# K evicted in output order, another unit order, gated loads and more filler matmuls in a fused attention and token-mixing kernel

## The chip, the cores and the metric

The kernel runs on one core of one Trainium2 chip. TensorE (PE) multiplies matrices into PSUM, VectorE (DVE) and ScalarE (ACT) read PSUM and write SBUF, GpSimd (POOL) works on SBUF and issues the input loads, SyncE (SP) issues the other transfers. Each engine works through its own queue in order. The metric is the device time of one execution in microseconds, the median of the runs; smaller is better.

## The reference, cut to what matters

Four batches of eight heads, 768 rows of 64. An 8x8 matrix P per head is normalised five times by rows and columns; it mixes the eight blocks of K and V. Block-local attention follows, then a token-mixing layer on the joined heads.

```python
P = sort_net
for _ in range(5):
    P = P - np.max(P, axis=-1, keepdims=True)
    P = np.exp(P)
    P = P / (np.sum(P, axis=-1, keepdims=True) + 1e-09)
    P = P / (np.sum(P, axis=-2, keepdims=True) + 1e-09)
k_sorted = np.einsum('bhij,bhjcd->bhicd', P, k_b).reshape(B, H, S, D)
v_sorted = np.einsum('bhij,bhjcd->bhicd', P, v_b).reshape(B, H, S, D)
...
scores = scale * np.matmul(q_b, k_sb.transpose(0, 1, 2, 4, 3))
attn = softmax(scores)          # per block of 96 rows
x = np.matmul(attn, v_sb)       # heads joined to [B, 768, 512]
...
wq = x @ w_q
wk = x @ w_k
W_tok = (1 / 8) * np.einsum('bsd,btd->bst', wq, wk)
mixed = np.einsum('bst,btd->bsd', W_tok, x)
out = np.maximum(mixed, 0.0) @ w_out
```

## The kernel before, in words

The whole kernel is a list of small units, written in the string `ORDER`. A unit is a letter, a batch, a number and one last character: `k02A` is unit k of batch 0, part 2, on ACT. A capital letter is a group of matmuls and its last character is the PSUM bank (0 to 7) that it starts at; a small letter is the work on A (ACT), D (DVE), P (POOL) or S (SP) that follows. The program walks the string and issues each unit in that order, so that the string sets the order on every engine's queue. All matmuls are issued by one helper, all plain copies by another, so most rows of the profile carry the helper's line.

For each batch the units are:

- `l`: a load on POOL's queue, which also converts fp32 to bf16: parts 0, 1, 2 are Q, K, V (1.5 MB read, 768 KB written), parts 3 and 4 the weights. Q, K and V have three buffers each (`NIN = 3`), so those of batch 3 wait until batch 0's are read.
- `c`, `i`: the Sinkhorn rounds on 32 rows and the constants. `U`, `b`, `B`, `n`, `u` turn the result into the matrices M that mix blocks (two buffers; batch 0's by DVE, the others by POOL).
- `Q`, `q`: 48 transposes of Q and their eviction into QT.
- `K`, `k`: for a pair of heads, 12 matmuls give the mixed and transposed K in PSUM, laid out as (r, s, i), 6 x 16 x 8; the eviction at the line of `copy` puts it into KT as (i, s, r), so that each block of 96 rows is contiguous. There are four such units in a batch.
- `V`, `v`, `R`: mixed V, its eviction, and a transfer on SP's queue that spreads it into VT.
- `S`, `e`: scores for five pairs of block and heads and their exp into E; seven units. `P`, `r`, `x`: attention times V, the reciprocal of the sums, and the product into X; five units.
- `T`, `t`, `J`, `j`, `d`, `W`, `w`, `G`, `g`, `H`, `h`, `O`, `o`, `y`: the token-mixing layer, transposes, projections, ReLU, the output product and its store.
- `Z`: filler matmuls of zeros, 128x512, whose result nobody reads. The number of matmuls is the number of the unit.

The loop that reads the string takes the second character as the batch and all between it and the last one as the number:

```python
for item in ORDER.split():
    kind, b, n, arg = item[0], int(item[1]), int(item[2:-1]), item[-1]
```

Of the kernel before, what the change touches and what calls it, by code (L numbers as in the profile page):

```python
# [9 lines left out]
BF16 = mybir.dt.bfloat16  # L10
# [5 lines left out]


ORDER = """
l00P l02P l01P i00P i03P i02P l03P l10P l11P l12P l04P l20P l21P l22P c00D Z087 c01D i01D c02D Z067
c03D Q027 Q016 c04D Q005 l30P q02D c05D q00D U004 b00D q01D B007 n01D n00D K020 u00D n11P K032 n10P  # L20
k02A V000 k03A K014 v00D V022 R00S k01D K000 l31P R01S v02A V016 l32P k00D R04S n20P v01A R05S S050
S062 S044 n21P e05A R03S S026 R02S e04A Q101 Q110 e02A q10D S034 q11D Q121 e06A S016 e03A P032 q12D
e01A r03D K120 x03D P024 k12A P016 r02D K112 x02D K100 k11A r01D T025 x01D k10A V122 t02A V110 v12D
T014 v11A K136 t01D R15S P042 R14S k13A S004 R13S V100 r04D x04D R12S e00A S166 n31P v10D S122 e16A
S144 n30P e12A P006 R11S S130 R10S r00D e14A T033 x00D Q222 e13A Q205 q22D T004 q20A S116 t03D S150
Q212 t00D e11A J013 q21D P124 e15A j01D K206 r12D d01S x12D P140 k20A K222 r14D P134 x14D k22A K216
r13D x13D P110 k21A W013 J002 r11D w01A x11D V204 j00A T123 d00S W002 v20D T137 w00A V220 t13A T112
t12D G006 R21S t11A v22D R20S S104 J113 e10A Q312 j11D R25S Q327 R24S q31A P100 d11S q32D K234 r10D
W117 x10D V212 k23A G016 w11A v21D S214 g01A S220 T107 e21A Q306 t10D R22S H012 e22A H004 R23S J107
h01D h00A K320 j10D S232 q30A O015 k32D d10S e23A V326 V310 o01A v32D S202 W104 v31A O025 R35S w10A  # L30
K306 R32S e20A o02D R33S G104 R34S k30A S250 P202 e25A O035 r20D x20D P216 o03A H020 G114 r21D y01S
h02A x21D S262 O005 g11A e26A O041 o00A H112 y00S T200 o04D P244 t20A h11D V306 O051 v30A r24D K332
x24D o05A R30S H126 R31S K314 k33D y02S h12A H100 k31D S242 h10A O157 e24A S314 S360 o15D O136 e36A
e31A P232 o13D S340 O107 r23D e34A x23D P224 o10A S320 O146 r22D e32A x22D T237 o14A S302 T225 t23D
e30A y12S P310 t22D S336 T214 r31D e33A P302 x31D J215 t21A r30D P326 x30D j21A S350 J204 d21S e35A
r32D W215 T303 x32D j20A O122 t30A d20S W204 w21A P330 o12D w20A T313 r33D G207 y11S x33D t31A P344
G217 O116 r34D g21A x34D T327 o11D T335 t32A H220 H212 t33D y10S J304 h22A h21D J315 H200 j30D O257
j31A h20D d30S d31S W316 W305 o25A O244 w30D w31A O205 o24A G307 y22S o20A O214 G317 o21A O225 g31D
y20S H320 O234 o22D h32A H302 H316 o23A O355 h31D h30A y21S O344 O307 O316 o30D o34A o35D O333 o31D
y32S O322 o33D y30S o32A y31S  # L40
"""


# [1 line left out]
def kernel(  # L45
# [11 lines left out]
    nc = tc.nc  # L57
    B, H, S, D = q.shape
    NB = sort_net.shape[-1]
    BLK = S // NB  # L60
    BH = B * H
    P = 128
    R6 = S // P
    SP = BLK // R6
# [16 lines left out]
    sb = ctx.enter_context(tc.tile_pool(name="sb", bufs=1))  # L81
    psp = ctx.enter_context(tc.tile_pool(name="psp", bufs=1, space=bass.MemoryType.PSUM))

    def tiles(name, n, shape, dtype=BF16):
        return [sb.tile(shape, dtype, name=f"{name}{i}") for i in range(n)]
# [16 lines left out]
    QT = tiles("QT", 2, [P, NP, R6, P])  # L102
    KT = tiles("KT", 2, [P, NP, S + P - BLK])
    Vs = tiles("Vs", 2, [P, R6, H, D1])
    VT = tiles("VT", 2, [BLK, NB, H * D1])
    E = tiles("E", 2, [BLK, NT, EW])
    X = tiles("X", 2, [BLK, NB, DM])
# [9 lines left out]
    R = tiles("R", 4, [BLK, 2, 7], FP32)  # L117
# [4 lines left out]
    tmp = sb.tile([BH, NB], FP32, name="tmp")  # L122
    idb = sb.tile([P, P], BF16, name="idb")
    m_p = sb.tile([P, SP], BF16, name="m_p")
    fil = sb.tile([P, 512], BF16, name="fil")

    Pv = Pm[:, 0:NB, :]
# [10 lines left out]
    def copy(e, o, i):  # L138
        if e == "A":
            nc.scalar.copy(o, i)  # L140
        else:
            nc.vector.tensor_copy(o, i)  # L142
# [99 lines left out]
    def flat(bank, nb=2):  # L242
        return PS[:, bank:bank + nb, :].rearrange("p a n -> p (a n)")
# [7 lines left out]
                   M[b % 2][:, h].rearrange("p s i -> p (s i)"))  # L251

    def u_k(b, n, e, bank):
        copy(e, KT[b % 2][:, n, 0:S].rearrange("p (i s r) -> p r s i", i=NB, s=SP),
             flat(bank)[:, 0:S].rearrange("p (r s i) -> p r s i", r=R6, s=SP))


    def u_V(b, n, bank):
# [9 lines left out]
    def u_R(b, n, e):  # L268
        ENG[e].dma_start(out=VT[b % 2].rearrange("(s r) i x -> r s i x", r=R6)[n],
                         in_=Vs[b % 2][:, n].rearrange("p h e -> p (h e)"))  # L270


    def u_S(b, n, bank):
# [16 lines left out]
    def grp(n):  # L290
        u0 = n * AG
        return u0, min(AG, NU - u0) // 2
# [117 lines left out]
    fills = dict(q="Q", k="K", v="V", e="S", r="P", x="P", t="T", j="J", w="W", g="G", h="H", o="O")  # L410
    for item in ORDER.split():
        kind, b, n, arg = item[0], int(item[1]), int(item[2:-1]), item[-1]
        if kind.isupper() and kind not in "R":
            banks[kind, b, n] = int(arg)
            if kind in "UB":
                U["t" if kind == "U" else "bank"] = int(arg)
            fns[kind](b, n, int(arg))
        elif kind in fills:
            src = (fills[kind], b, 1 if kind == "g" else n)
            fns[kind](b, n, arg, banks[src])  # L420
        else:
            fns[kind](b, n, arg)
# [30 lines left out]
```

## Time and profile before

| what | value |
|---|---|
| median of 3 runs | 160.85 us (158.92 to 160.88) |
| the profiled execution's own time | 161.63 us |
| its span, first to last instruction | 159.5 us |
| mean granted TensorE clock | 0.783 |
| loads of Q, K, V | 12, 768 KB each |
| filler matmuls | 14 |

The page gives busy time per engine, the span in 40 slices (tenths), the chain of work that ended last with its shares, and groups of instructions with their busy time, mean duration in ns of one, and the idle time ahead of them with what ended it. In slices of 4 us, DMA is full for the first 60 us, and PE has its longest idle stretches from 10 to 60 us.

### The profile page before, as it was taken

The numbers are of one execution on the slowest core, as the hardware profiler recorded it, in microseconds if no ns is written. First come the engines' busy times: TensorE is split into PE (matmuls) and PEld (weight loads), VectorE is DVE, ScalarE is ACT, GpSimd is POOL, SyncE is SP. The second block draws the span as 40 slices with busy tenths as digits, with TensorE's granted clock in tenths as the row PEclk, the third lists the DMA queues.
The fourth block names the chain that finished last, engine by engine and source line by source line (L and its number), as shares of the span: only waits on it lengthen the run. The fifth ranks groups of instructions, "written<-read, shape, count | busy, mean of one in ns | idle before, by whom it ended". The sixth has DMA issues, their size and how long they took to land.

```text
span 159.5 us, 3288 instructions
## 1 busy us (share of the span) xinstructions
PE 107.3 (67%) x1390; PEld 71.0 (45%) x1399; DVE 87.5 (55%) x130; ACT 101.1 (63%) x95; POOL 26.2 (16%) x37
## 2 busy tenths in 40 slices
PE   6561346197226499626797594859655999999960
PEld 2161335186126378524656443434313686644320
DVE  3888039838231535940447179433994886862360
ACT  3110695289997986799648972993923687553520
POOL 7998751900000600000000000000000000000000
PEclk9959555559855855975559879996975899999998
DMA  2999999999999990000230200415220031435545
GB/s 14 183 201 201 195 204 204 233 242 204 204 204 206 230 217 11 12 4 0 50 96 16 69 5 11 134 48 216 85 116 0 4 132 29 164 123 197 201 188 209
DMA packets 19950, 20.19 MB, mean 127 GB/s; under 512 B 2016, under 2 KB 18400, under 8 KB 19936
## 3 DMA queue, kind: packets, MB, share of 16 engines
q0 software_dynamic: 14064, 10.09, 42.1%
q1 hardware_dynamic: 5872, 9.89, 18.5%
q8 instruction: 11, 0.18, 0.5%
q14 instruction: 3, 0.02, 0.0%
HBM read 20.19 MB, written 6.29 MB: 166 GB/s over the span
## 4 chain that ended last, share of the span: by engine, by line
PE 46%; ACT 21%; DVE 12%; issue 9%; DMA 8%; POOL 1%; DVEq 0%; ACTq 0%; POOLq 0%
PE ps L136 46%; ACT KT L140 17%; DVE KT L142 11%; DMA Kn<-in_k_dram 8%; ACT E L284 3%; DVE Vs L142 1%; POOL Qn L99 1%; POOL Vn L99 1%; ACT ot L140 0%; ACT wk L140 0%; ACT Vs L140 0%; DVE qkT L142 0%; DVEq L142 0%; ACTq L140 0%; POOLq L437 0%
## 5 line engine op out<-in xcount | busy, mean ns | idle before, releaser
L140 ACT CAST KT<-ps 128x768 bf16<-128x768 f32 x11 | 42.4, 4101 | 8.5 <-PE ps L136 8.4
L284 ACT ACTIVATE E<-ps 96x960 bf16<-96x960 f32 (+1 forms) x28 | 24.9, 925 | 12.4 <-PE ps L136 12.0
L136 PE MATMUL ps<-wo,mixT 128*128 128x512 bf16 x87 | 25.5, 418 | 0.9 <-issue 0.5
L316 DVE TENSOR_TENSOR X<-ps,R 96x896 bf16<-96x896 f32 (+1 forms) x20 | 20.1, 1006 | 0.7
L136 PE MATMUL ps<-QT,KT 64*128 64x96 bf16 x256 | 11.4, 237 | 13.2 <-DVE KT L142 8.0
L142 DVE CAST KT<-ps 128x768 bf16<-128x768 f32 x5 | 19.3, 4025 | 0.4 <-PE ps L136 0.4
L136 PE MATMUL ps<-Vn,M 128*128 128x128 bf16 x96 | 10.4, 274 | 13.2 <-ACT KT L140 10.9
L142 DVE CAST Vs<-ps 128x1024 bf16<-128x1024 f32 x7 | 8.8, 1258 | 18.1 <-PE ps L136 18.1
L136 PEld LDWEIGHTS <-KT 64*128 64x128 bf16 x256 | 8.3, 112 | 16.9 <-issue 13.4
L136 PEld LDWEIGHTS <-M 128*128 128x128 bf16 x96 | 8.4, 125 | 14.8 <-issue 14.4
L136 PE MATMUL ps<-M,Kn 128*64 128x128 bf16 x192 | 9.8, 251 | 7.7 <-ACT KT L140 4.8
L136 PE MATMUL ps<-VT,E 96*128 96x65 bf16 x256 | 12.4, 202 | 2.2 <-ACT KT L140 2.0
L136 PEld LDWEIGHTS <-mixT 128*128 128x128 bf16 x96 | 8.5, 103 | 10.7 <-issue 3.0
L142 DVE COPY ot<-ps 128x512 f32<-128x512 f32 x11 | 7.6, 711 | 9.8 <-PE ps L136 9.8
L136 PEld LDWEIGHTS <-E 96*128 96x128 bf16 x256 | 10.7, 103 | 4.8 <-issue 3.4
L136 PE MATMUL ps<-idb,Qn 128*64 128x128 bf16 x192 | 10.5, 292 | 2.8 <-POOL E L183 2.7
L140 ACT COPY ot<-ps 128x512 f32<-128x512 f32 x13 | 7.6, 587 | 6.9 <-PE ps L136 5.0
L136 PEld LDWEIGHTS <-Kn 128*64 128x64 bf16 x192 | 7.2, 127 | 10.5 <-issue 6.9
L216 POOL TENSOR_TENSOR M<-PTR,m_p 128x512 bf16<-128x512 bf16 x6 | 7.7, 1312 | 21.7 <-PE ps L136 21.6
L136 PEld LDWEIGHTS <-Qn 128*64 128x64 bf16 x192 | 9.2, 158 | 4.5 <-DMA Qn<-in_q_dram 3.2
L136 PE MATMUL ps<-idb,X 96*128 96x96 bf16 x128 | 10.0, 235 | 1.3 <-ACT wk L140 1.3
L311 DVE RECIPROCAL R<-ps 96x14 f32<-96x14 f32 (+1 forms) x20 | 4.6, 229 | 10.5 <-PE ps L136 10.4
(64 smaller groups left out, 131.7 us busy)
## 6 DMA issues: line engine op xcount, KB each, us to landing
out_dram<-ot SPq DMA_DIRECT2D x12, 512.0 KB, 2.9
VT<-Vs SPq DMA_DIRECT2D x24, 130.0 KB, 3.9
Qn<-in_q_dram POOLq DMA_DIRECT2D x4, 768.0 KB, 17.3
Vn<-in_v_dram POOLq DMA_DIRECT2D x4, 768.0 KB, 23.3
Kn<-in_k_dram POOLq DMA_DIRECT2D x4, 768.0 KB, 19.8
wo<-in_moe_w_out_dram POOLq DMA_DIRECT2D x1, 512.0 KB, 20.2
qD<-qkT SPq DMA_DIRECT2D x8, 48.0 KB, 1.9
wqk<-in_moe_w_q_dram POOLq DMA_DIRECT2D x1, 64.0 KB, 7.5
```

The lines of the kernel that those rows point to most:

```text
L99: nc.gpsimd.dma_start(out=t[b % NIN].rearrange("p h r d -> p h (r d)"), in_=src[b].rearrange("h (p r) d -> p h (r d)", p=P))
L136: nc.tensor.matmul(o, w, x, is_transpose=t, start=start, stop=stop, skip_group_check=True)
L140: nc.scalar.copy(o, i)
L142: nc.vector.tensor_copy(o, i)
L216: ENG[e].tensor_tensor(out=M[b % 2][:, h0:h1], in0=src.unsqueeze(2).to_broadcast([P, 4, SP, NB]), in1=m_p.unsqueeze(1).unsqueeze(3).to_bro ...
L284: nc.scalar.activation(E[b % 2][:, n, 0:2 * w * BLK].rearrange("p (t a c) -> p a t c", a=2, c=BLK), PS[0:BLK, bank:bank + 2, 0:w * BLK].re ...
L311: nc.vector.reciprocal(rr[b, n][:, :, 0:w], avps(bank, w)[:, :, :, D])
L316: nc.vector.tensor_mul(xo.rearrange("p (a t d) -> p a t d", a=2, d=D), avps(bank, w)[:, :, :, 0:D], rr[b, n][:, :, 0:w].unsqueeze(3).to_br ...
```

## The change

The eviction of K walks the same elements in the order of the output in place of that of the input. The order of all units is another one. Loads after the first four wait for gates: a unit `N` copies one element of a tile into a scrap tile on POOL, so that what stands behind it in POOL's queue goes out only when that tile's unit has run. The queue of loads begins q, k, v where it was q, v, k, and batch 1's K follows at once. There are more filler units: 14 groups with 64 matmuls in place of 2 groups with 14. Evictions are dealt out anew: K 9 on ACT and 7 on DVE (before 11 and 5), Q 6 and 6 (3 and 9), V 6 and 6 (5 and 7), output 16 and 8 (13 and 11), the ReLU 8 and 4 (7 and 5), the projections 2 and 6 (4 and 4), and all 8 of `w` on DVE (1).

```diff
-l00P l01P l02P i00P i03P i02P l03P l10P l11P l12P l04P l20P l21P l22P c00D Z087 c01D i01D c02D Z067
...
+l00P l01P l02P i00P i03P i02P l11P c00D Z087 c01D i01D c02D Z027 c03D Z127 c04D Q026 Q007 q02D c05D
...
+R00S K112 S000 R04S S044 n20P e00A k11D S066 e06A R02S K100 e04A S012 R05S S036 R03S k10A Z1125 Z924
+e03A K120 K134 e01A k12D S026 e02A k13D P002 S050 r00D Z1227 e05A x00D N00x l21P P014 V106 r01D P030
...
+    gate = sb.tile([1, 1], BF16, name="gate")
...
     def u_k(b, n, e, bank):
-        copy(e, KT[b % 2][:, n, 0:S].rearrange("p (i s r) -> p r s i", i=NB, s=SP),
-             flat(bank)[:, 0:S].rearrange("p (r s i) -> p r s i", r=R6, s=SP))
+        copy(e, KT[b % 2][:, n, 0:S].rearrange("p (i s r) -> p i s r", i=NB, s=SP),
+             flat(bank)[:, 0:S].rearrange("p (r s i) -> p i s r", r=R6, s=SP))
...
+    def u_N(b, n, e):
+        t = dict(q=QT, k=KT, v=Vs, e=E, x=X)[e][b % 2]
+        if e == "q":
+            src = t[0:1, 0, 2 * n + 1, P - 1:P]
+        elif e == "k":
+            src = t[0:1, n, S - 1:S]
+        elif e == "v":
+            src = t[0:1, 2 * n + 1, H - 1, D - 1:D]
+        elif e == "e":
+            src = t[0:1, n, 0:1]
+        else:
+            src = t.rearrange("p i m -> p (i m)")[0:1, grp(n)[0] * D:grp(n)[0] * D + 1]
+        nc.gpsimd.tensor_copy(gate, src)
...
-        if kind.isupper() and kind not in "R":
+        if kind.isupper() and kind not in "RN":
```

On ACT, the rows from the start of batch 0 to its first exps. Before (the table of exp is loaded first, Pm is the Sinkhorn matrix; a row with x2 stands for two alike):

```order
L155 ACT_TABLE_LOAD
L155 ACTIVATE Pm<-Pm 32x64 x5
L140 CAST KT_79<-ps 128x6x16x8 x2
L140 CAST Vs_81<-ps 128x8x2x64 x2
L284 ACTIVATE E_85<-ps 96x2x5x96 x3
L284 ACTIVATE E_85<-ps 96x2x2x96
```

And in the changed kernel, the same place on ACT:

```order
L157 ACT_TABLE_LOAD
L157 ACTIVATE Pm<-Pm 32x64 x5
L142 COPY QT_77<-ps 128x4x256
L142 CAST PTR<-ps 128x256
L142 CAST KT_79<-ps 128x768 x2
L142 CAST Vs_81<-ps 128x8x2x64
L142 CAST KT_79<-ps 128x768
L301 ACTIVATE E_85<-ps 96x2x5x96
L301 ACTIVATE E_85<-ps 96x2x2x96
```

One eviction of Q, the copy PTR of the block matrices and a third eviction of K came to ACT there, a V went to DVE, and the write of KT is one run of 768.

On POOL, the rows behind the constants, before (Qn, Kn and Vn are the loaded tiles; M_105 is batch 1's M):

```order
L190 DMA wqk<-in_moe_w_q_dram 128x4x64
L190 DMA wqk<-in_moe_w_k_dram 128x4x64
L99 DMA Qn_67<-in_q_dram 128x8x384
L99 DMA Kn_70<-in_k_dram 128x8x384
L99 DMA Vn_73<-in_v_dram 128x8x384
L192 DMA wo<-in_moe_w_out_dram 128x4x512
L99 DMA Qn_68<-in_q_dram 128x8x384
L99 DMA Kn_71<-in_k_dram 128x8x384
L99 DMA Vn_74<-in_v_dram 128x8x384
L99 DMA Qn_66<-in_q_dram 128x8x384
L216 TENSOR_TENSOR M_105<-PTR,m_p 128x512 x2
```

And in the changed kernel, the same place on POOL, from the second gate on to the loads of batches 2 and 3:

```order
L287 COPY gate<-KT_79 1x1
L100 DMA Vn_73<-in_v_dram 128x8x384
L100 DMA Qn_67<-in_q_dram 128x8x384
L218 TENSOR_TENSOR M_104<-PTR,m_p 128x512 x2
L287 COPY gate<-X_87 1x1
L100 DMA Kn_71<-in_k_dram 128x8x384
L287 COPY gate<-QT_78 1x1
L100 DMA Qn_68<-in_q_dram 128x8x384
L100 DMA Kn_69<-in_k_dram 128x8x384
L194 DMA wo<-in_moe_w_out_dram 128x4x512
L100 DMA Vn_72<-in_v_dram 128x8x384
L100 DMA Qn_66<-in_q_dram 128x8x384
```

Each COPY gate stands ahead of the loads that it holds back: one on batch 0's X, then one on batch 1's QT ahead of five loads. The load of batch 2's V (Vn_74) is still further behind, after a gate on batch 2's E.

More of the change, by code (lines that the diff above doesn't have):

```diff
@@ L18 @@
 ORDER = """
[L19 to L38, printed above, removed]
@@ L39 @@
-y20S H320 O234 o22D h32A H302 H316 o23A O355 h31D h30A y21S O344 O307 O316 o30D o34A o35D O333 o31D
-y32S O322 o33D y30S o32A y31S
+l00P l01P l02P i00P i03P i02P l11P c00D Z087 c01D i01D c02D Z027 c03D Z127 c04D Q026 Q007 q02D c05D
+Q015 Z224 q01A q00D U006 Z423 b00D Z322 B003 n00D u00A Z522 n11P n01D Z622 K010 K032 n10P k01A K024
+k03D Z727 k02A N02k l03P Z1026 V000 V022 v00A K004 v02D V016 k00A N00k l12P l10P Z821 R01S n21P v01D
+R00S K112 S000 R04S S044 n20P e00A k11D S066 e06A R02S K100 e04A S012 R05S S036 R03S k10A Z1125 Z924
@@ new lines @@
+e03A K120 K134 e01A k12D S026 e02A k13D P002 S050 r00D Z1227 e05A x00D N00x l21P P014 V106 r01D P030
+x01D v10A P042 r04D P024 r03D x04D T007 x03D V112 t00A R10S v11A r02D Q106 x02D R11S Q127 T031 q12A
+Q110 q10D T015 t03D q11A N11q l20P l31P l04P l32P l30P T024 V122 t01A S100 n31P v12D S156 t02A J005
+e10A n30P S122 R12S j00D J014 R15S e15A K200 R14S j01D W005 R13S e12A w00D W014 S116 w01D G005 e11A
+K232 G015 k23A K216 g01D k20A k21D S144 P112 e14A P100 r11D K226 x11D P134 k22A r10D Q213 r13D x10D
@@ new lines @@
+S166 Q202 q21A x13D T101 q20A Q220 t10D S134 e16A q22D e13A K322 P146 k32D S250 S214 e25A r14D P122
+x14D e21A K330 r12D S246 d00S x12D k33A K304 e24A k30D S220 T123 T112 e22A t12D K314 S236 t11D T133
+k31A S260 J102 t13D e23A S204 d01S j10D J113 e26A N26e l22P e20A V306 V310 v30D j11A W102 H024 v31A
+W113 w11D V326 w10D h02D G103 v32A H000 d10S R30S Q312 h00D Q325 q31A G113 q32D Q304 g11A H010 O057
+q30D h01A S312 o05D S324 e31A S330 O036 R34S e32A R35S V222 o03D R33S O007 e33A v22D R32S d11S V214
@@ new lines @@
+R31S V200 o00D v21A R25S S342 O016 R24S v20D e34A R23S H114 R22S O027 o01D R20S R21S H100 P322 o02A
+h11D y00S O046 h10A r32D S304 x32D y01S o04A O107 e30A P240 y02S P232 o10A r24D P214 x24D P226 r23D
+r21D O131 x23D O120 r22D o13A x21D T233 o12A P201 x22D t23A S364 y11S O110 e36A r20D T223 x20D o11A
+T217 P304 t22A y10S T202 r30D t21A H120 x30D J213 t20A P316 j21D h12A S354 J202 r31D d21S x31D e35A
+W213 O141 j20D T300 w21D o14A d20S P334 t30D W207 P342 r33D O156 w20D x33D G207 o15A r34D T311 x34D
@@ L41 @@
+T320 y12S t31A G217 t32D T336 g21A J301 t33D H222 H214 j30D J310 h22A d30S W301 H206 j31A w30D O243
+h20A d31S W312 G301 o24D h21A O250 w31D O227 o25A G311 y22S o22A O230 g31A H302 H324 o23A O211 h32A
+y21S H316 O200 o21D O351 h30D h31A O345 o20A o35D O314 y20S o34D O307 o31A y32S O325 o30A O334 y30S
+o32A o33A y31S
 """
```

## The prediction

> **What bounds the kernel now.** I read the page first, from its busy line and slices down to its chain, then the waits, then the groups with their shapes kept apart, and last the timeline and the stretches.
>
> ```profile
> PE 107.3 (67%) x1390; PEld 71.0 (45%) x1399; DVE 87.5 (55%) x130; ACT 101.1 (63%) x95; POOL 26.2 (16%) x37
> ...
> PEclk9959555559855855975559879996975899999998
> DMA  2999999999999990000230200415220031435545
> ...
> PE 46%; ACT 21%; DVE 12%; issue 9%; DMA 8%; POOL 1%; DVEq 0%; ACTq 0%; POOLq 0%
> PE ps L136 46%; ACT KT L140 17%; DVE KT L142 11%; DMA Kn<-in_k_dram 8%; ACT E L284 3%; DVE Vs L142 1%; POOL Qn L99 1%; POOL Vn L99 1%; ACT ot L140 0%; ACT wk L140 0%; ACT Vs L140 0%; DVE qkT L142 0%; DVEq L142 0%; ACTq L140 0%; POOLq L437 0
> ```
>
> No engine is full. The chain is PE for 46% and the eviction of K into KT for 28%, on two engines. The slices say the same: the granted clock drops to 5 wherever PE waits, and it waits for the evictions:
>
> ```profile
> PE ps L136 <- ACT KT L140: 25.1, 10, 3.4
> ...
> PE ps L136 <- DVE KT L142: 10.3, 4, 3.5
> ```
>
> That is 35.4 us of PE standing idle (total, times, longest). The eviction is dear by its shape:
>
> ```profile
> L140 ACT CAST KT<-ps 128x768 bf16<-128x768 f32 x11 | 42.4, 4101 | 8.5 <-PE ps L136 8.4
> L142 DVE CAST KT<-ps 128x768 bf16<-128x768 f32 x5 | 19.3, 4025 | 0.4 <-PE ps L136 0.4
> ...
> L142 DVE CAST Vs<-ps 128x1024 bf16<-128x1024 f32 x7 | 8.8, 1258 | 18.1 <-PE ps L136 18.1
> ...
> L140 ACT CAST Vs<-ps 128x1024 bf16<-128x1024 f32 x5 | 5.1, 1029 | 5.1 <-PE ps L136 5.1
> ...
> L142 DVE CAST qkT<-ps 128x384 bf16<-128x384 f32 x4 | 2.2, 556 | 2.9 <-PE ps L136 2.9
> ...
> L140 ACT CAST qkT<-ps 128x384 bf16<-128x384 f32 x4 | 1.9, 476 | 0.5 <-PE ps L136 0.5
> ```
>
> A cast of 1024 elements from the same memory costs 1029 ns on ACT and 1258 on DVE, the KT cast of only 768 costs four times that on both engines. Both write KT in steps of 96 elements, two bytes at a time.
>
> **The change part by part.** *The eviction.* Writes become contiguous; the step moves to the read, innermost six elements 512 bytes apart in PSUM. For a contiguous 768 I interpolate between the rows for 384 and 1024: ACT 476 + 384 x (1029 - 476)/640 = 808 ns, DVE 556 + 384 x (1258 - 556)/640 = 977 ns. Whether a stepped read is dearer, DVE shows in one place:
>
> ```profile
> L142 DVE COPY ot<-ps 128x512 f32<-128x512 f32 x11 | 7.6, 711 | 9.8 <-PE ps L136 9.8
> ...
> L216 DVE TENSOR_TENSOR M<-ps,m_p 128x512 bf16<-128x512 f32 x2 | 1.3, 669 | 0.0
> ```
>
> The M multiply reads 512 fp32 of PSUM 128 bytes apart and takes 669 ns, no more than the contiguous copy of 512 (711). ACT has no such row. So the ends are 0.81/0.98 us, and 4.1 us if the stepped read costs what the stepped write did; I take the low end, since the nearest row shows no price for the step at all. The Trainium skill speaks against this: "SBUF — State Buffer", in the note on cachelines under "Door 1: The DMA port swizzle", says that PSUM has 8-byte lines and that each access into a new line pays a penalty, and the new read changes its line at every element. By that rule the eviction would stay dear; the 669 ns row does not bear it out for DVE, and no row here shows it for ACT. It gives the first rival below.
>
> With 9 evictions on ACT and 7 on DVE, ACT's 42.4 us become 7.3 and DVE's 19.3 become 6.8. On the chain 28% of 159.5 = 44.7 us shrink to about 0.22 of that: 34.9 us leave.
>
> *What is late next* is PE itself. Its work at full clock is 107.3 us times the mean clock:
>
> ```profile
> core 0: 159.5 us, clock 0.783
> ```
>
> = 84.0 us. This holds 14 filler matmuls.
>
> *The fillers.* They go from 14 to 64. Eleven groups have 2, one has 8, but the reader of the table takes everything between the second character and the last as the count, so Z1125 gives 12 matmuls and Z1227 gives 22. The price of a 128x512 matmul stands in the timeline at half and at full clock (start, us):
>
> ```profile
> 106.94 3.20 PE L136 MATMUL ps<-wo,mixT 128*128 128x512 bf16 x8
> ...
> 148.66 5.35 PE L136 MATMUL ps<-wo,mixT 128*128 128x512 bf16 x23
> ```
>
> 0.40 and 0.23 us. The first 30 fillers stand where PE waits for the Sinkhorn chain, M or the loads; about nothing of them is on the path, 1 us if that cover is thin. The 12 and the 22 stand in batch 0 between scores and attention: 2.8 and 5.1 us at full clock, 4.8 and 8.8 at half. PE being next in line, I count them in full, at full clock because they follow one another.
>
> *The loads.* The queue now runs q0, k0, v0, k1, and everything after that waits for gates.
>
> ```profile
> DMA to landing us min/median/max: 7.6/17.3/31.9
> ...
> 3.17 13.37 DMA Kn<-in_k_dram
> ...
> 13.87 1.27 DVE L216 TENSOR_TENSOR M<-ps,m_p 128x512 bf16<-128x512 f32 x2
> ...
> VT<-Vs SPq DMA_DIRECT2D x24, 130.0 KB, 3.9
> ...
> 0.31 0.11 POOL L437 MEMSET const-bfloat16-1.0<- 128x1 bf16 x1
> ```
>
> The first load (Qn, issued at 1.25) lands 7.6 us later, at 8.85; the third, issued at 3.17, at 16.54; so a load takes 3.85 us in the queue and k0, now second, lands at 12.7. M is ready only at 15.1, so K starts there, 1.5 us earlier than now. A gate is one GpSimd copy of one element; the nearest row is the 0.11 us memset, the far one M's multiply of 1.31 us. What counts is what queues behind it on POOL: the next loads and the M multiplies of later batches, and behind those PE.
>
> *Batch 0.* v0 lands third at 16.6. The last KT eviction stands behind v00 on ACT: 16.6 + 0.6 (V) + 1.0 + 0.6 (K) + 0.8 = about 20. Scores and the exps e00, e06, e04, 2.8 us, give 22.9; the 12 fillers, whose bank e04 frees, end at 25.7. The last V eviction ends near 20.5, two VT issues and 3.9 us of transfer later, 25.5, VT is there, so it is not late. Four small units, the first P and e02's bank: 28.6. The 22 fillers: 33.7.
>
> *From there on PE is the bound.* Done by then are Q, K, V and S of batch 0, K of batch 1 and one P; by these rows
>
> ```profile
> 83.09 1.25 PE L136 MATMUL ps<-idb,Qn 128*64 128x128 bf16 x32
> ...
> 84.83 0.53 PE L136 MATMUL ps<-M,Kn 128*64 128x128 bf16 x12
> ...
> 85.58 0.62 PE L136 MATMUL ps<-Vn,M 128*128 128x128 bf16 x8
> ...
> 125.52 0.62 PE L136 MATMUL ps<-VT,E 96*128 96x65 bf16 x14
> 126.07 0.39 PE L136 MATMUL ps<-QT,KT 64*128 64x96 bf16 x10
> ```
>
> 48 x 0.039 + 96 x 0.044 + 24 x 0.078 + 64 x 0.039 + 0.6 = 11.1 us. Left: 84.0 - 3.2 (old fillers) - 11.1 = 69.7. How well PE keeps going without KT waits shows in the last two stretches before the end (us, then busy time of PE, PEld, DVE, ACT, POOL; clock):
>
> ```profile
> 90.00:122.00 32.00, 22.59 (x265) 12.09 (x268) 21.45 (x17) 20.04 (x23) 0.00 (x0) 0.82 0.23 78
> 122.00:151.00 29.00, 28.55 (x327) 16.54 (x332) 17.83 (x27) 18.43 (x28) 0.00 (x0) 0.96 0.31 117
> ```
>
> From 122 on, with the last KT eviction gone, PE is idle 0.45 us of 29; from 90 to 122 over 9 of 32. I take 10%, 7 us (ends 2% and 25%: 1.4 and 17). ACT and DVE have then 74 and 76 us of work in all, each below PE. The end:
>
> ```profile
> 154.09 0.58 ACT L140 COPY ot<-ps 128x512 f32<-128x512 f32 x1 [1.88 <-PE ps L136]
> ```
>
> From 154.0 to the span's 159.5 pass 5.5 us, as before; the time of this execution, 161.63, is 2.1 over its span.
>
> Sum: 33.7 + 69.7 + 7 + 5.5 + 2.1 = 118.0. The other way round, from the chain: 161.6 - 34.9 + 7.9 (both large groups) = 134.6 if the new order and the warmer clock give nothing, 126.7 if those fillers are hidden. The PE sum gets more weight, because the chain's 46% of PE holds matmuls at half clock behind the waits that leave: 120. Its own range is 116 to 125. The profiled 161.63 is 0.8 us above the median of 160.85; I leave that inside the range.
>
> **The rivals.**
>
> *The stepped read costs what the stepped write did* (the other side). Place: the 16 KT evictions; speaking for it, the same 768 elements and a step of 512 bytes, and ACT without a row; against it, the 669 ns. The chain keeps its 44.7 us and PE gets 7.9 us of fillers: 161.6 + 7.9 = 169.5, slower. It decides from about 3.3 us per eviction on, where 10.9 evictions on the chain (44.7/4.1) save no more than the fillers cost. This is also what the cachelines note of the Trainium skill would give, at its strongest. Chance 0.03. Halfway, at 2 us an eviction, 10.9 x 1.1 = 12 us come on top of 120: 132, chance 0.07.
>
> *Late loads take the place of the evictions.* The gate behind q11 opens near 40: 33.7, then some 6 us of P, X, T, V and Q before q11 is evicted. Behind it stand q2, k3, wo, v3 and q3: the first lands 7.6 us on, at 48, then one each 3.85 us (wo, two thirds of the bytes, 2.6): 52, 54, 58, 62. Counted by the units between them in the new order at the rows' durations, PE comes to q3 some 23 us of work after the gate, at 63 to 65, and v2, gated on e26 near 60, lands near 68 when PE wants it. There is almost no slack. Should the transfers cross the VT scatters, or a gate open late, 3 to 12 us of waiting and of cold clock follow: 123 to 132, middle 127. Chance 0.24. For it speaks the median of 17.3 us to landing; against it, that this median comes from nine loads queued at once.
>
> *PE hardly waits at all:* 2% in place of 10%, and the 12 fillers hidden behind the exps: 118.0 - 5.6 - 1 = 111 to 116. For it the stretch from 122 on; against it, that this stretch has no loads and no evictions. Chance 0.16.
>
> **How the numbers follow.** Likeliest, the PE sum with a modest share of waiting, 116 to 125: chance 0.50, so 120. Late loads 0.24, PE without waits 0.16, halfway eviction 0.07, stepped read as dear as the write 0.03. From 113 to 132 leaves out the low end of one, part of the halfway case and the slow rival, some 0.18. A measurement here tells 2% from no change. Faster by over 2% hold all cases but the last: 0.96; within 2%, 0.01 between the halfway case and the slow one; slower 0.03.
>
> **What would show it.** KT<-ps near 0.8 us on ACT and 1.0 on DVE, and no KT among PE's longest waits; PE at over 80% of the span with a granted clock near 0.9; the fil group with 64 matmuls, its last 22 ending near 34 us; k0 landing at 12.7; the first K matmul at 15. Wrong would be: KT over 2 us, PE waiting long for Qn, Kn or Vn between 45 and 70 us, or the clock at half through the 22 fillers.

## The result and the profile after

The changed kernel takes 123.98 us, the median of 4 runs (123.15 to 125.23), beside 160.61 us for the kernel before in the same comparison. The ratio is 0.771, with a 95% interval of 0.765 to 0.778. The profiled execution is the longest of the four, 125.23 us with a span of 123.3. Runs more than 1.5% above the fastest of their kernel count as slow and are left out of the ratios; the profiled executions of the changed kernel and of two below, one VT gate and no late fillers, are such runs.

The page of the changed kernel, its busy line, the slices of the clock and of the transfer engines, and the groups that matter (line, engine, operation, out<-in, count, then busy us and mean ns of one, then the idle time ahead):

```profile
span 123.3 us, 3389 instructions
...
PE 101.9 (83%) x1439; PEld 65.7 (53%) x1449; DVE 69.5 (56%) x132; ACT 69.2 (56%) x93; POOL 27.1 (22%) x42
...
PEclk9976999999679999995589999999999999999995
DMA  0999999899949426999999339947947104144493
...
L142 ACT CAST KT<-ps 128x768 bf16<-128x768 f32 x9 | 7.1, 800 | 6.8 <-PE ps L138 6.8
...
L144 DVE CAST KT<-ps 128x768 bf16<-128x768 f32 x7 | 6.6, 956 | 6.7 <-PE ps L138 6.5
```

The eviction of K fell from 4101 to 800 ns on ACT and from 4025 to 956 on DVE. ACT and DVE together lost 61.7 - 13.7 = 48 us of busy time on it. PE is now busy for 83% of the span, and the clock stands at 9 but for a few slices, from 31 to 37 us and from 55 to 65 above all. The long waits for KT are gone from the list of PE's waits; at its top stands one that the kernel before did not have at all (us in total, times, longest):

```profile
PE ps L138 <- DMA VT<-Vs: 7.2, 2, 4.5
```

PE's own timeline shows where these two waits lie, and the fillers beside them (start, us, and in brackets the idle time ahead and what ended it):

```profile
24.21 3.18 PE L138 MATMUL ps<-fil 128*128 128x512 bf16 x13 [0.18 <-ACT E L301]
...
31.23 0.61 PE L138 MATMUL ps<-VT,E 96*128 96x65 bf16 x14 [2.72 <-DMA VT<-Vs]
...
33.04 5.60 PE L138 MATMUL ps<-fil 128*128 128x512 bf16 x20 [0.22 <-issue]
38.48 0.62 PE L138 MATMUL ps<-VT,E 96*128 96x65 bf16 x14
...
55.85 1.70 PE L138 MATMUL ps<-VT,E 96*128 96x65 bf16 x28 [4.53 <-DMA VT<-Vs]
...
112.38 6.22 PE L138 MATMUL ps<-wo,mixT 128*128 128x512 bf16 x27
```

Batch 0's attention waits for VT until 31.2, the 22 fillers fill PE until 38.5, and batch 1's attention waits for VT again until 55.9. From there on PE hardly stops, and from 70 us on it runs at full clock. Two stretches of the same view as before the change (start and end, length in us, busy time of PE, PEld, DVE, ACT and POOL, clock, DMA share, GB/s) say so:

```profile
70.00:90.00 20.00, 19.48 (x293) 12.49 (x295) 15.16 (x23) 14.52 (x19) 1.12 (x2) 1.00 0.80 193
90.00:118.00 28.00, 27.63 (x286) 15.42 (x288) 16.17 (x29) 18.40 (x28) 0.00 (x0) 1.00 0.37 142
```

So the time fell by 160.61 - 123.98 = 36.6 us, close to the 34.9 that were to leave the chain, and what bounds the kernel now is PE's own work behind two waits for transfers.

### The profile page after: what moved, and what is told of

Read it like the earlier page. It is cut to its first block, busy times and chain, and to the rows that moved or that the text cites. A ratio compares the mean times of both kernels' runs of the same rounds, so it can differ in the third digit from the quotient of the medians.

```text
span 123.3 us, 3389 instructions
## 1 busy us (share of the span) xinstructions
PE 101.9 (83%) x1439; PEld 65.7 (53%) x1449; DVE 69.5 (56%) x132; ACT 69.2 (56%) x93; POOL 27.1 (22%) x42
## 5 line engine op out<-in xcount | busy, mean ns | idle before, releaser
L138 PE MATMUL ps<-wo,mixT 128*128 128x512 bf16 x90 | 22.6, 380 | 0.6 <-issue 0.2
L333 DVE TENSOR_TENSOR X<-ps,R 96x896 bf16<-96x896 f32 (+1 forms) x20 | 19.7, 998 | 0.5
L138 PE MATMUL ps<-fil 128*128 128x512 bf16 x60 | 17.6, 438 | 2.0 <-DVE fil L153 1.2
L138 PEld LDWEIGHTS <-E 96*128 96x128 bf16 x256 | 10.3, 103 | 9.4 <-issue 8.5
L142 ACT COPY ot<-ps 128x512 f32<-128x512 f32 x16 | 9.4, 585 | 10.1 <-PE ps L138 9.2
L138 PEld LDWEIGHTS <-fil 128*128 128x128 bf16 x64 | 6.5, 110 | 10.0 <-issue 4.4
L142 ACT CAST KT<-ps 128x768 bf16<-128x768 f32 x9 | 7.1, 800 | 6.8 <-PE ps L138 6.8
L142 ACT CAST Vs<-ps 128x1024 bf16<-128x1024 f32 x6 | 6.2, 1029 | 8.1 <-PE ps L138 7.8
L144 DVE CAST KT<-ps 128x768 bf16<-128x768 f32 x7 | 6.6, 956 | 6.7 <-PE ps L138 6.5
L144 DVE COPY ot<-ps 128x512 f32<-128x512 f32 x8 | 5.5, 689 | 7.6 <-ACT ot L142 4.8
L406 ACT ACTIVATE mixT<-ps 128x1024 bf16<-128x1024 f32 x8 | 8.1, 1029 | 2.7 <-PE ps L138 2.6
L144 DVE CAST Vs<-ps 128x1024 bf16<-128x1024 f32 x6 | 7.2, 1222 | 3.0 <-PE ps L138 3.0
```

The costliest lines, as they stand in the source:

```text
L138: nc.tensor.matmul(o, w, x, is_transpose=t, start=start, stop=stop, skip_group_check=True)
L333: nc.vector.tensor_mul(xo.rearrange("p (a t d) -> p a t d", a=2, d=D), avps(bank, w)[:, :, :, 0:D], rr[b, n][:, :, 0:w].unsqueeze(3).to_br ...
L406: nc.scalar.activation(o, i, ACT.Relu)
```

## The experiments

Each kernel ran beside the kernel before on the same chip; ratios are to that one. First the table, then each with its edit and what was expected of it.

| kernel | median us | ratio to before, 95% interval |
|---|---|---|
| changed kernel | 123.98 | 0.771 (0.765 to 0.778) |
| eviction alone | 124.01 | 0.774 (0.764 to 0.783) |
| eviction undone | 150.14 | 0.940 (0.929 to 0.951) |
| small filler groups | 121.77 | 0.765 (0.760 to 0.770) |
| one VT gate | 128.28 (lowest 125.13) | none given |
| no gates | 124.07 | 0.779 (0.773 to 0.785) |
| VT first | 125.11 | 0.787 (0.782 to 0.792) |
| steps of six | 135.14 (one run) | none given |
| no late fillers | 121.24 | 0.756 (0.748 to 0.763) |
| loads between | 117.89 | 0.736 (0.732 to 0.740) |
| no late fillers, no gates | 120.75 | 0.754 (0.750 to 0.759) |

### The eviction alone

The kernel before, with these two lines only:

```diff
-        copy(e, KT[b % 2][:, n, 0:S].rearrange("p (i s r) -> p r s i", i=NB, s=SP),
-             flat(bank)[:, 0:S].rearrange("p (r s i) -> p r s i", r=R6, s=SP))
+        copy(e, KT[b % 2][:, n, 0:S].rearrange("p (i s r) -> p i s r", i=NB, s=SP),
+             flat(bank)[:, 0:S].rearrange("p (r s i) -> p i s r", r=R6, s=SP))
```

> The kernel before with the new eviction of K and nothing else. Theory (the eviction is the gain, by the chain): KT<-ps near 0.80 us on ACT and 0.96 on DVE, the 34.9 us leave the chain less a few that other waits take: 127 to 138 us. Rival (the new order carries the gain): over 145 us, with KT just as short.

It took 124.01 us, below the range of the theory and far from the rival's: two lines give all of the change's gain, 0.774 against 0.771 with intervals that overlap. Order, gates, the new dealing of evictions and fillers together add nothing to it that can be measured. The old order then has the same wait, only longer, and its queue of loads keeps the transfer engines full from 3 to 60 us (slices of 3 us). In PE's list of waits and the page of this kernel:

```profile
PE ps L136 <- DMA VT<-Vs: 10.3, 2, 5.7
```
```profile
PE 92.6 (77%) x1390; PEld 62.5 (52%) x1399; DVE 72.7 (60%) x130; ACT 67.0 (56%) x95; POOL 26.2 (22%) x37
...
PEclk9999955897555999977999999999999999999995
DMA  0999999999999999999952316447012144165193
```

PE works 9.3 us less here than in the changed kernel (92.6 against 101.9), which has 50 more fillers, and waits more: 10.3 us for VT in place of 7.2.

### The eviction undone

The changed kernel with the two lines set back.

> The changed kernel with the old eviction, all else as changed. Theory: KT<-ps at 4.0 to 4.1 us again, 16 evictions of which some 11 end a wait: 155 to 175 us, no faster than before. Rival (order, gates and fillers carry the gain): under 140 us.

Both missed: 150.14 us, 6% faster than before, not slower. The mean of one eviction was 4021 ns on ACT and 3966 on DVE, as expected. The new order deals them out 9 and 7 in place of 11 and 5, and PE waits for them less:

```profile
PE ps L138 <- ACT KT L142: 12.4, 7, 2.7
...
PE ps L138 <- DVE KT L144: 3.3, 2, 2.9
```

PE waits 12.4 + 3.3 = 15.7 us for KT, where it was 35.4. So the new list of units, with its dealing, fillers and gates, is worth 159.70 - 150.14 = 9.6 us as long as the eviction is dear, and nothing measurable once it is cheap. Which of its parts brings the 9.6 us was not tested. The two gains do not add up, because they take away the same wait: the new list 19.7 us of it, and the cheap eviction alone all but 0.7.

### Smaller filler groups

```diff
-R00S K112 S000 R04S S044 n20P e00A k11D S066 e06A R02S K100 e04A S012 R05S S036 R03S k10A Z1125 Z924
+R00S K112 S000 R04S S044 n20P e00A k11D S066 e06A R02S K100 e04A S012 R05S S036 R03S k10A Z125 Z924
-e03A K120 K134 e01A k12D S026 e02A k13D P002 S050 r00D Z1227 e05A x00D N00x l21P P014 V106 r01D P030
+e03A K120 K134 e01A k12D S026 e02A k13D P002 S050 r00D Z127 e05A x00D N00x l21P P014 V106 r01D P030
```

> The changed kernel with the groups of 12 and 22 fillers cut to 2 each. Theory: the 20 matmuls of the second stand on PE's path, 20 x 0.23 = 4.7 us less; the first group hides behind PE's wait for VT of batch 0 and gives nothing: 118.5 to 120.5 us. Rival (they pay by keeping the clock up): the clock falls to half between 30 and 40 us and the time stays within 1.5 us of the changed kernel, or gets longer.

121.77 us, 2.2 us less than the changed kernel by the medians: neither the 118.5 to 120.5 us of the theory nor the rival's 1.5 us or less, and the intervals of the two ratios overlap (0.760 to 0.770, 0.765 to 0.778). The timeline shows where the gain came from and where part of it went:

```profile
31.06 0.93 PE L138 MATMUL ps<-VT,E 96*128 96x65 bf16 x14 [4.58 <-DMA VT<-Vs]
...
33.26 0.98 PE L138 MATMUL ps<-VT,E 96*128 96x65 bf16 x14 [0.22 <-issue]
...
51.92 1.70 PE L138 MATMUL ps<-VT,E 96*128 96x65 bf16 x28 [4.69 <-DMA VT<-Vs]
```

The first group was hidden, as expected: the wait for batch 0's VT grew from 2.7 to 4.6 us and ended at the same time. The second was on the path: the next P starts at 33.3 in place of 38.5. Of these 5.2 us 3.9 are left when the second VT wait ends: up to that wait PE is now busy for 13.6 us at a mean granted clock of 0.90 (33.3 to 47.2 us), where the changed kernel needs 12.4 us at 1.00 (38.5 to 51.3).

### No late fillers

All fillers behind the first 12 are taken out of the string; the gates stay.

> The changed kernel with only its first 12 fillers, the other 52 gone. Theory (they cost their length where PE is the bound and buy little clock): the same as with the small groups within 1 us, 120.5 to 123 us. Rival (the fillers between the units of batch 0 are worth having): the granted clock from 15 to 34 us falls to about 0.5 to 0.6 and the time is 123.5 us or more.

121.24 us, in the range of the theory. Ratios 0.756 and, with the small groups, 0.765 have intervals that overlap and leave open whether the small groups cost anything. Against the changed kernel's 0.771 the intervals are just apart (0.748 to 0.763, 0.765 to 0.778): the late fillers as a whole cost some 2.5 us. The rival named the right event and the wrong price: the granted clock from 15 to 31 us does fall, from 1.00 to 0.71, but that stretch ends with the wait for VT, which lasts until 31.4 us here and until 31.2 in the changed kernel.

### No gates

The five `N` units are taken out of the changed kernel.

> The changed kernel without its five gate copies; each load goes out as soon as its place in POOL's queue and its buffer allow. Theory (VT's transfers share the transfer engines with the loads that are in flight): more loads stand in flight when batch 0's VT is sent, PE's wait for VT grows from 7.2 to 9 to 12 us, time 125 to 129 us. Rival (the gates do nothing, or hold the loads back at a cost): 122 to 124.5 us, PE waiting for VT no longer than now.

The rival holds: 124.07 us, and PE waits 7.3 us for VT, as with the gates (7.2). By 30 us POOL has issued eight loads behind batch 1's K, where the changed kernel has issued two, and the two waits for VT are 4.0 and 3.2 us (2.7 and 4.5 with the gates): more loads in the queue do not make PE wait longer. With the late fillers gone as well:

> The changed kernel with only its first 12 fillers and without the five gates: what the new order of units and the new eviction give by themselves. Theory (the gates do nothing, the late fillers cost 2 to 3 us): 120 to 122 us, as with the gates. Rival (gates and fillers need each other): 123 us or more, or below 119.

120.75 us, as with the gates (121.24). So the gates of the change neither help nor harm by any amount that shows, with the late fillers or without, and the new order without gates and late fillers is 2.5% ahead of the old order with the same eviction (0.754 against 0.774).

### One gate on VT

K, V and Q of batch 3 and the output weights behind a gate that reads all six parts of batch 1's VT; Q of batch 2 stays where it was.

```diff
-Q110 q10D T015 t03D q11A N11q l20P l31P l04P l32P l30P T024 V122 t01A S100 n31P v12D S156 t02A J005
+Q110 q10D T015 t03D q11A N11q l20P T024 V122 t01A S100 n31P v12D S156 t02A J005
...
-e10A n30P S122 R12S j00D J014 R15S e15A K200 R14S j01D W005 R13S e12A w00D W014 S116 w01D G005 e11A
+e10A n30P S122 R12S j00D J014 R15S e15A K200 R14S j01D W005 R13S N10r l31P l04P l32P l30P e12A w00D W014 S116 w01D G005 e11A
...
+        if e == "r":
+            src = t[0:R6, 0, 0:1]
```

> The changed kernel with batch 3's K, V, Q and the output weights held back until batch 1's VT has landed; only batch 2's Q goes out at the old gate. Theory (the six VT transfers of batch 1 are late because five loads fill the same engines): PE's wait for VT near 51 to 56 us falls from 4.5 to 1 to 2.5 us, and if batch 3's loads still come in time the time is 121 to 122.5 us. Rival (the transfers are slow by themselves): the wait stays over 4 us. Second rival: the wait goes, but Kn or Qn of batch 3 come late by as much and the time stays at 124.

The first rival's number came: the second wait for VT only fell from 4.53 to 4.06 us, with four of five loads held back, and PE then waited 3.0 us for Vn. The times, 125.1 to 129.9 us, are no better than the changed kernel's. Since batch 2's Q was still in flight beside VT, this run does not tell a transfer that is slow by itself from one that is slowed by a load; the next kernel does.

### VT first

The kernel with the small filler groups, in which V and Q of batch 1 wait for all of batch 0's VT and the five next loads for all of batch 1's.

```diff
-k03D Z727 k02A N02k l03P Z1026 V000 V022 v00A K004 v02D V016 k00A N00k l12P l10P Z821 R01S n21P v01D
-R00S K112 S000 R04S S044 n20P e00A k11D S066 e06A R02S K100 e04A S012 R05S S036 R03S k10A Z125 Z924
+k03D Z727 k02A N02k l03P Z1026 V000 V022 v00A K004 v02D V016 k00A Z821 R01S n21P v01D
+R00S K112 S000 R04S S044 n20P e00A k11D S066 e06A R02S K100 e04A S012 R05S S036 R03S N00r l12P l10P k10A Z125 Z924
...
-Q110 q10D T015 t03D q11A N11q l20P l31P l04P l32P l30P T024 V122 t01A S100 n31P v12D S156 t02A J005
-e10A n30P S122 R12S j00D J014 R15S e15A K200 R14S j01D W005 R13S e12A w00D W014 S116 w01D G005 e11A
+Q110 q10D T015 t03D q11A T024 V122 t01A S100 n31P v12D S156 t02A J005
+e10A n30P S122 R12S j00D J014 R15S e15A K200 R14S j01D W005 R13S N10r l20P l31P l04P l32P l30P e12A w00D W014 S116 w01D G005 e11A
```

> The kernel with the small filler groups (121.8 us), and V and Q of batch 1 held back until all of batch 0's VT has landed, the five loads for batches 2 and 3 until all of batch 1's VT has landed. Theory: with nothing else in flight VT lands some 2.5 us after its last issue, PE's waits for VT fall from 9.3 to under 4 us, and the time to 116 to 119 us. Rival (as with the one gate before): the loads come late by as much, PE waits for Qn, Kn or Vn instead, and the time stays at 121 to 125 us.

Half of each came: the waits for VT went, as in the theory, and V and Q came late, as in the rival; the time is just above the rival's range. In PE's timeline:

```profile
27.67 0.61 PE L138 MATMUL ps<-VT,E 96*128 96x65 bf16 x14 [0.85 <-DMA VT<-Vs]
...
35.56 1.01 PE L138 MATMUL ps<-Vn,M 128*128 128x128 bf16 x8 [5.98 <-DMA Vn<-in_v_dram]
...
50.41 1.06 PE L138 MATMUL ps<-VT,E 96*128 96x65 bf16 x28 [0.21 <-ACT KT L142]
...
58.05 1.06 PE L138 MATMUL ps<-idb,Qn 128*64 128x128 bf16 x16 [5.57 <-DMA Qn<-in_q_dram]
```

The waits for VT are nearly gone (0.85 us, then none, where the kernel with small groups had 9.3), and 6.0 and 5.6 us of waiting for V and Q stand in their place; the median is 125.11 us. This shows that a load in flight slows VT. The rows of SP's queue give the end of batch 0's six issues, in the changed kernel first, then in this one; PE's timeline gives the landing:

```profile
19.48 4.13 SPq L271 DMA_DIRECT2D VT<-Vs  x6
```
```profile
20.34 3.92 SPq L271 DMA_DIRECT2D VT<-Vs  x6
```

23.6 to 31.2 is 7.6 us with loads in flight; 24.3 to 27.7 is 3.4 us without. In the changed kernel batch 1's V, issued at 20.7 us, lands 9.9 us later, so it is in flight for most of that time, with Q queued behind it. Six times 130 KB beside one 768 KB load take about twice the time. Loads queued behind that one do not add to it, as the kernel without gates showed; there the loads issued at 21.3, 24.7, 25.6 and 26.5 us land at 35.0, 38.9, 42.8 and 46.8, one every 3.9 us, so they move one after another. The Trainium skill says in "Trainium Kernel Development and Optimization", under "Key Constraints", that transfers issued from the SP, ACT and POOL queues all run on the same 16 engines and interleave; the 7.6 against 3.4 us agree.

### Loads set between the VT transfers

If VT and the load beside it are wanted at the same moment, holding either back helps nothing; the load has to move in the idle time of the transfer engines (slices 12 and 14 to 16 of the changed kernel: 4, 4, 2 and 6). Here K and Q of batch 2 go out as soon as batch 0's VT has landed, V and Q of batch 1 only after batch 0's second V eviction, and the loads of batch 3 and the output weights after batch 1's VT. No fillers behind the first 12; the edit is shown against that kernel.

```diff
-k03D k02A N02k l03P V000 V022 v00A K004 v02D V016 k00A N00k l12P l10P R01S n21P v01D
-R00S K112 S000 R04S S044 n20P e00A k11D S066 e06A R02S K100 e04A S012 R05S S036 R03S k10A e03A K120 K134 e01A k12D S026 e02A k13D P002 S050 r00D e05A x00D N00x l21P P014 V106 r01D P030
+k03D k02A N02k l03P V000 V022 v00A K004 v02D V016 k00A R01S n21P v01D N01v l12P l10P
+R00S K112 S000 R04S S044 n20P e00A k11D S066 e06A R02S K100 e04A S012 R05S S036 R03S N00r l21P l20P k10A e03A K120 K134 e01A k12D S026 e02A k13D P002 S050 r00D e05A x00D P014 V106 r01D P030
...
-Q110 q10D T015 t03D q11A N11q l20P l31P l04P l32P l30P T024 V122 t01A S100 n31P v12D S156 t02A J005
-e10A n30P S122 R12S j00D J014 R15S e15A K200 R14S j01D W005 R13S e12A w00D W014 S116 w01D G005 e11A
+Q110 q10D T015 t03D q11A T024 V122 t01A S100 n31P v12D S156 t02A J005
+e10A n30P S122 R12S j00D J014 R15S e15A K200 R14S j01D W005 R13S N10r l31P l04P l32P l30P e12A w00D W014 S116 w01D G005 e11A
```

> The kernel with only its first 12 fillers (121.2 us), and the loads set between the VT transfers: V and Q of batch 1 go out when batch 0's second V eviction is done, K and Q of batch 2 when batch 0's VT has landed, the loads of batch 3 and the output weights when batch 1's VT has landed. Theory (a VT transfer and the load in flight share the engines, and both are wanted at the same moment; so fetch the load in the idle transfer time before it): PE's waits for VT fall from 9.8 to 2 to 5 us without a new wait for Qn, Kn or Vn over 2 us, and the time to 115.5 to 118.5 us. Rival (what is taken from one wait comes back in another, as in the kernel with VT first): 120 to 123 us.

117.89 us, in the theory's range, and the ratio of 0.736 lies clear of all others. POOL issues batch 1's V at 21.6 us, behind four of the six VT issues (20.7 us in the changed kernel, behind two), and batch 2's Q at 30.6 us in place of 45.7. In PE's timeline:

```profile
29.22 0.93 PE L137 MATMUL ps<-VT,E 96*128 96x65 bf16 x14 [2.20 <-DMA VT<-Vs]
...
46.02 1.06 PE L137 MATMUL ps<-VT,E 96*128 96x65 bf16 x28 [1.13 <-ACT E L302]
...
54.48 0.53 PE L137 MATMUL ps<-M,Kn 128*64 128x128 bf16 x12 [3.60 <-DMA Kn<-in_k_dram]
```

One VT wait of 2.2 us is left, the second is gone; K of batch 3 now comes 3.6 us late, more than the 2 us that the theory allowed. This kernel is 4.5% faster than the changed one, by 0.736/0.771, and 2.6% faster than the same one without late fillers, by 0.736/0.756.

### Steps of six

The eviction in the order i, r, s, so that writes lie 12 bytes apart, and reads 32.

```diff
-        copy(e, KT[b % 2][:, n, 0:S].rearrange("p (i s r) -> p i s r", i=NB, s=SP),
-             flat(bank)[:, 0:S].rearrange("p (r s i) -> p i s r", r=R6, s=SP))
+        copy(e, KT[b % 2][:, n, 0:S].rearrange("p (i s r) -> p i r s", i=NB, s=SP),
+             flat(bank)[:, 0:S].rearrange("p (r s i) -> p i r s", r=R6, s=SP))
```

> The changed kernel with the eviction walking KT in the order i, r, s: two-byte writes 12 bytes apart, reads 32 bytes apart. If the dear thing is any write that is not next to the last one: KT<-ps near 4.0 us as before. If it is only a step as large as 192 bytes: near 0.8 to 1.0 us. In between if neighbouring writes within a short piece are cheaper.

In between, and nearer to the dear end:

```profile
L142 ACT CAST KT<-ps 128x768 bf16<-128x768 f32 x9 | 24.3, 2781 | 5.4 <-PE ps L138 5.4
L144 DVE CAST KT<-ps 128x768 bf16<-128x768 f32 x7 | 18.9, 2737 | 6.7 <-PE ps L138 6.7
```

2781 and 2737 ns, where the contiguous write takes 800 and 956 and the write in steps of 192 bytes 4021 and 3966 (eviction undone). The read has a step here too, 32 bytes. That the price is the write's is argued from the changed kernel, whose read steps by 512 bytes and shows no price. The time in its one run is 135.14 us.

## Why the prediction was right, and where it was off

The forecast was 120.0 us with a range of 113 to 132; measured were 123.98. What was right is the price of the eviction, the wait that leaves with it, and PE as the next bound. One step of the path failed, that VT is not late, and it pushed two terms of the sum up. The sum itself was 118.0, 6 us below the measured time, and the forecast came nearer because 2 us were added in view of the chain, for a reason that has nothing to do with VT: that part is luck. The measured time lies in the range of the likeliest case (116 to 125) and in that of the late loads (123 to 132), so the number alone does not decide between them; the traces do, as follows.

*The eviction.* 808 and 977 ns were forecast, 800 and 956 measured. No price of the stepped read is seen on either engine, so the row of the M multiply was the right one to go by. The cachelines note that the prediction cited from the Trainium skill states the penalty for a new line of SBUF, and of PSUM that non-contiguous access slows matmuls; as a rule for these reads it is not borne out: 768 fp32 of PSUM, each in a new line, take what the interpolated contiguous cast takes. Its other half, that a new 16-byte line of SBUF has a price, agrees with the writes: 192 bytes apart the dearest, 12 bytes apart, where most writes change the line, in between.

*34.9 us off the chain.* The eviction alone gave 159.7 - 124.0 = 35.7 us by the medians.

*The 22 fillers end at 33.7.* They ended at 38.5, where the next P starts. This is the first term that was too small. The step "25.5, VT is there, so it is not late" failed: VT was there at 31.2. I took 3.9 us for a VT transfer from the page before, its median over all 24, while V of batch 1 was in flight beside these six; from the last issue on it took 7.6 us, and SP's six issues lasted until 23.6, 2.4 us past the last V eviction, where two issues were allowed for. The 12 fillers thereby lost their price, as the small groups showed. The 22 began at 32.2 in place of 28.6 and took 6.3 us in place of 5.1; 20 of them took 5.6 us, 0.28 each where 0.23 was taken, at a mean granted clock of 0.80 from 33.0 to 38.6 us.

*PE from there on.* 69.7 us of work and 7 us of waiting were forecast, 76.7 in all; from the second P's start at 38.5 to the last matmul's end at 118.6 it took 80.1. By the view of stretches PE is busy for 73.9 us of that time and idle for 6.2, 4.5 of these at the second VT wait, so the 7 us of waiting were enough. What was too small is the work, where 69.7 us were taken at full clock: right behind that wait the granted clock is 0.50, and from 60 to 70 us 0.87.

```profile
55.80:60.00 4.20, 4.15 (x70) 3.79 (x70) 2.17 (x5) 0.80 (x1) 0.00 (x0) 0.50 1.28 207
```
```profile
60.00:70.00 10.00, 9.63 (x209) 7.70 (x206) 8.14 (x13) 8.84 (x11) 0.00 (x0) 0.87 1.13 176
```

An estimate from these two rows, busy time times what the clock lacks to 1: 4.15 x 0.50 + 9.63 x 0.13 = 3.3 us of the 4.2 by which the work was over. The late-loads rival had the right neighbourhood ("should the transfers cross the VT scatters") and the lower clock, and the wrong victim: PE waited for no Q, K or V between 45 and 70 us, what came late was VT, and the gates were not its cause, since without them PE waited for it as long.

*The end.* 118.6 to 123.3 is 4.7 us (5.5 forecast), and the time is 1.9 us over the span (2.1). Summed again with the measured terms: 38.5 + 80.1 + 4.7 + 1.9 = 125.2, the time of the profiled execution, which is 1.3 us above the median.

*A rival's price.* For a stepped read as dear as the stepped write the prediction gave 169.5 us, slower than before. With the eviction undone the same kernel took 150.1. I had left the evictions on the chain as they were and put the fillers on top, while the new list of units more than halves PE's wait for them. The chance of 0.03 for slower stood on a price that was too high.

*What the prediction did not ask* is which part of the change brings the gain. It expected the order to be worth something next to the short eviction; the runs show that with the change's fillers in it, it is worth nothing measurable, and 2.5% without the late ones and the gates.

## What to carry to other kernels

When an eviction has to permute, let the step fall on the PSUM read and keep the SBUF write contiguous; a row of the same operation with the same step on either side prices this ahead of time. When a large wait goes, look for what the transfers were doing under its cover: a median time to landing does not hold where a load is in flight beside the transfer. A filler matmul is work like any other once PE is the bound, and a count that a parser reads out of a table should be checked against the instruction list.

## What the runs showed of the hardware

An eviction of 768 elements per partition from fp32 PSUM to two bytes in SBUF costs about the same on ACT and DVE: 4.0 us with writes 192 bytes apart, 2.7 to 2.8 us with writes 12 bytes apart (and reads 32), 0.8 and 0.96 us with writes side by side, though the reads then step by 512 bytes. A transfer from SP's queue is slowed by one load in flight (7.6 against 3.4 us for 780 KB), and not further by the loads that queue behind it: PE waited 7.2 us for VT with the gates and 7.3 us without. After PE had waited 4.5 us for VT, its granted clock was 0.50 for the next 4 us in the changed kernel, and 0.50 as well behind the 4.7 us of the kernel with small filler groups.
